# v of pair 0 loaded by units, an earlier first part of W_in, v narrowed on GpSimd, and a last result in three pieces

## The chip, the cores and the metric

The kernel runs on one core of one Trainium2 chip. The core has five engines with instruction streams of their own: TensorE (PE, with its weight loads as PEld), VectorE (DVE), ScalarE (ACT), GpSimd (POOL) and SyncE (SP). SP and POOL issue the DMAs here; 16 DMA engines move the data. The metric is the device time of one execution in microseconds (us). The kernel before takes 178.17 us (median of 4 runs, 178.02 to 178.48).

## The reference

A gated recurrence over 768 steps, for 4 batches and 8 heads of width 48, whose output feeds a two-layer network:

```python
for t in range(S):                                   # B, H, S, D = 4, 8, 768, 48
    state = alpha[:, :, t, :, None] * state + einsum('bhd,bhe->bhde', k[:, :, t], v[:, :, t])
    y[:, :, t] = einsum('bhd,bhde->bhe', q[:, :, t], state)
x = y.transpose(0, 2, 1, 3).reshape(3072, 384)
h = x @ w_in                                         # 384 x 2048
g = 0.5 * h * (1 + tanh(c * (h + 0.044715 * h ** 3)))
out = g @ w_out                                      # 2048 x 384, float32
```

## The kernel before

**Tiling.** The 768 steps are cut into 6 chunks of 128 steps. Two batches of one chunk are a *pair*; there are 12 pairs, numbered 0 to 11 (pairs 0 and 1 are chunk 0, pairs 2 and 3 chunk 1, and so on). One batch of a pair is a *unit*, 0 or 1. For a pair the kernel loads a (alpha), q, k and v, takes the logarithm of a (`ln`), sums it along the steps by a matmul (`cum`), and exponentiates the sums (`b`, `binv`, `bend`). Then q and k are scaled (`qp`, `kp`), turned over on PE (`t`) and copied out of PSUM (`ev`), multiplied (`attn`) and masked (`mask`). `y` is the masked product times v, plus the part that comes from the state; `x` copies it to bf16, `tx` turns it over, `xe` copies that into `xT`. `kv` and `st` carry the state on; from chunk 1 on `st` is two VectorE instructions (L520 adds, L523 multiplies), in chunk 0 it is one. `end` prepares the factor of `st`.

**The two layers.** `l1` (L564) is 6 matmuls of 128x256, 8 such tasks for each pair (`l10.` to `l111.`), and `gelu` (L570) follows on ACT. `l2` (L583) multiplies by W_out, 4 tasks of 4 matmuls of 128x384 for each unit; `ot` (L595) copies the result out of PSUM and `store` (L601) writes it. The tasks `l20.` are the second layer of pairs 0 and 1 together (16 tasks); they begin when all 16 `l1` tasks of these two pairs have been issued. W_in comes in four parts, each read by two `l1` tasks of every pair: part 0 by `l1` 0 and 1, part 1 by 2 and 3, part 2 by 4 and 5, part 3 by 6 and 7. W_out comes in four parts too.

**Packed pairs.** Pairs 0 and 1 are loaded in a layout of their own (q, k and a by unit on SP, L297), so that their `kp` is not in the order that `kv` needs; k is turned back (`t0.4`, `t0.5`, `t1.4`, `t1.5` with their `ev`, L446 and L453). Their v is loaded as float32 (L300) and narrowed to bf16 by `vb` (L381), on ACT or VectorE. Later pairs' v is narrowed by the DMA itself.

**The last unit.** Its second layer is done in two halves of 192 columns, each over all 16 blocks of the inner dimension, in a bank of its own, with its own `ot` and `store` (32 matmuls of 128x192).

**What sets the order.** Everything is a task with dependencies, buffers that it takes, and costs; `Scheduler.order` lays the tasks out on engines, and every engine then runs its own list in order. First it takes the steps of `FIRST`, a list written out by hand (engine:task, `fill.n` being n matmuls on zeros); after that it chooses by due times and by the costs `W`. While it goes through `FIRST` it uses the costs of the table `COST` where that has an entry. `LANDED` holds the due times of the loads, `LOADS` the order in which POOL issues them, and a `gate` is a tiny POOL copy (L306) that holds the POOL queue until a load has landed or a task is done. A POOL load also waits until the eighth load before it on POOL has landed. The PSUM pool `yk` has two buffers, shared by `t`, `kv`, `y` and `tx`; `ff` has four, for `l1`, `l2`, the fills and, in pairs 0 and 1, `cum`.

POOL's order before is: gate on a of pair 0, unit 1; v of pair 0 in one load; gate on `qp` of pair 0, unit 1; W_in part 0; v of pair 1; W_in parts 1, 2, 3; W_out parts 0, 1; then a, q, k, v of the first unit of pair 2; W_out part 2; and so on.

Of the kernel before, what the change touches and what calls it, by code (L numbers as in the profile page):

```python
# [16 lines left out]
    cum=530, cum_packed=1500, t8=450, t4=225, attn=340, kv=170, inter=170, intra=205, tx=168, l1_4=655, l1_2=340, l2=655,  # L17
    qk2=910, qk1=500, ev8=650, ev4=350, mask=640, st=1090, st0=545, end=110, attn2=590, vb=320, vb_act=480, ring=1300, ring_issue=670, out=2050, lead=600, receipt=1400, receipt_hw=1000, xc=520, xe=330, ot=540,
    ev8_act=960, ev4_act=520, xc_act=450, xe_act=450, ot_act=450,
# [5 lines left out]
    ("DVE", "ev"): (605, 115), ("DVE", "kp"): (480, 120), ("DVE", "mask"): (605, 115), ("DVE", "qp"): (480, 120),  # L25
    ("DVE", "st"): (470, 130), ("DVE", "x"): (480, 120), ("DVE", "xe"): (270, 120),
}
LAT = {"SP": 0, "PE": 210, "ACT": 110, "DVE": 90, "POOL": 0}
# [18 lines left out]
class Scheduler:  # L47
# [16 lines left out]
    def order(self):  # L64
        free = {e: 0 for e in LAT}
        taken = {tag: [] for tag in self.bufs}
        table, wire, xbar, head, out = LN_EXP, 0, 0, 0, []
# [26 lines left out]
        def put(t, at, e):  # L94
            nonlocal wire, xbar
            for tag, users in t.takes:
                taken[tag].append(users)
            cost, lat = COST.get((e, t.kind), (t.cost[e], LAT[e])) if fixed else (t.cost[e], LAT[e])
            t.start, t.end, t.engine, t.load = at, at + cost, e, None
            free[e] = t.end  # L100
            t.done = t.end + lat
            if t.name in self.landed:
                t.done = self.landed[t.name]
                if e != "SP":
                    wire = t.done - W["receipt"]
            elif t.land is not None:
                wire = max(wire, t.end + W["lead"]) + t.land
                t.done = wire + W["receipt_hw" if e == "SP" else "receipt"]
            if t.kind in ("turn", "store"):
                xbar = t.done = max(xbar, t.end + W["landed"] - t.xbar) + t.xbar  # L110
                t.done += t.late
            out.append(t)
# [59 lines left out]
class _Kernel:  # L172
# [5 lines left out]
    EARLY = (0, 1)  # L178
    LOADS = ('gatea 0 1', 'v0', 'gateqp 0 1', 'in 0', 'v1', 'in 1', 'in 2', 'in 3', 'out 0', 'out 1', '2a', 'out 2', '2b', 'out 3', '3', '4', '5', '6', '7', '8', '9', '10', '11')

# [3 lines left out]
    FIRST = """  # L184
        A:table.0 S:load.0 S:load.1 S:load.2 S:load.3 S:load.4 A:ln0.0 S:load.5 P:fill.7 P:cum0.0 A:ln0.1 G:gate.0 G:load.12 S:load.6 P:cum0.1 A:b0.0 S:load.7
        A:binv0.0 V:qp0.0 A:bend0.0 A:b0.1 V:kp0.0 S:load.8 P:fill.2 P:t0.0 A:bend0.1 A:binv0.1 V:ev0.0 P:t0.1 S:load.9 A:ev0.1 S:load.10 V:qp0.1 P:fill.3
        P:attn0.0 V:kp0.1 P:t0.2 G:gate.1 S:load.11 G:load.13 V:mask0.1 P:fill.1 P:t0.3 G:load.14 A:ev0.3 V:end0.0 V:ev0.2 A:ln1.0 V:mask0.0 P:fill.4
        P:attn0.1 G:load.15 P:cum1.0 V:mask0.2 A:vb0.0 G:load.16 A:ln1.1 V:vb0.1 P:y0.0 V:mask0.3 A:b1.0 P:cum1.1 G:load.17 A:x0.0 V:qp1.0 A:binv1.0 P:y0.1
        G:load.18 A:b1.1 P:t1.0 V:x0.1 A:bend1.0 G:load.19 A:ev1.0 V:kp1.0 P:fill.2 P:tx0.1 V:xe0.1 A:binv1.1 P:tx0.0 G:load.20 P:t1.1 A:bend1.1 V:xe0.0
        G:load.21 V:qp1.1 P:t0.5 A:ev1.1 V:kp1.1 G:load.22 A:ev0.5 P:fill.1 P:attn1.0 G:load.23 P:t1.3 V:mask1.1 P:t1.2 A:ev1.3 P:l10.0 G:load.24 V:mask1.0  # L190
        A:ev1.2 P:kv0.1 G:load.25 V:end1.0 V:st0.1 P:t0.4 G:load.26 P:attn1.1 A:ev0.4 P:t1.5 G:load.27 A:ev1.5 V:vb1.0 G:load.28 V:mask1.2 P:y1.0 P:l10.1
        G:load.29 A:x1.0 V:mask1.3 A:vb1.1 P:kv0.0 P:tx1.0 G:load.30 V:st0.0 P:l10.3 V:xe1.0 P:y1.1 P:kv1.1 G:load.31 P:l10.2 V:x1.1 A:gelu0.0 V:st1.1 P:tx1.1
        A:gelu0.1 G:load.32 P:l10.4 V:xe1.1 A:gelu0.3 P:l10.5 A:gelu0.2 G:load.33 P:l11.0 A:gelu0.4 A:gelu0.5 P:l11.1 A:gelu1.0 P:l11.2 A:gelu1.1 P:l11.6
        A:gelu1.2 P:l10.6 A:gelu1.6 P:l11.5 A:gelu0.6 P:l11.7 A:gelu1.5 P:l11.4 A:gelu1.7 P:l10.7 A:gelu1.4 P:l11.3 A:gelu0.7 P:t1.4 A:gelu1.3 P:l20.1 V:ev1.4
        P:l20.2 P:kv1.0 P:l20.5
    """.split()
    LANDED = {"load.0": 2800, "load.1": 3400, "load.2": 4400, "load.3": 5100, "load.4": 6750, "load.5": 7300, "load.12": 9850, "load.6": 9000, "load.7":
              10300, "load.8": 10800, "load.9": 11300, "load.10": 11900, "load.11": 12300, "load.13": 14900, "load.14": 17600, "load.15":
              19300, "load.16": 21300, "load.17": 23000, "load.18": 25000, "load.19": 26600, "load.20": 27700, "load.21": 28400, "load.22":
              29000, "load.23": 29400, "load.24": 31300, "load.25": 32100, "load.26": 32700, "load.27": 33300, "load.28": 33800, "load.29":  # L200
              35900, "load.30": 37700, "load.31": 39400, "load.32": 41300, "load.33": 42600}

# [7 lines left out]

    HALVES = ((3, 0), (3, 1), (3, 2), (3, 3), (4, 0))

# [54 lines left out]
    def copy(self, e):  # L267
        return self.nc.scalar.copy if e == "ACT" else self.nc.vector.tensor_copy

# [303 lines left out]
    def layer2(self, f, c, b, part):  # L573
        def emit(e):
            if part == 0:
                f["acc", c, b] = self.tile("ff", [self.C, self.d_model], F32, "acc")
            if part == 2 and (c, b) == (self.NCH - 1, self.B - 1):
                f["acc", c, b] = self.tile("ff", [self.C, self.d_model], F32, "acc")
            last, w = (c, b) == (self.NCH - 1, self.B - 1), self.d_model // 2
            for lo, hi, nts in (((part // 2 * w, part // 2 * w + w, range(part % 2 * 8, part % 2 * 8 + 8)),) if last else  # L580
                                ((0, self.d_model, range(part * 4, part * 4 + 4)),)):
                for nt in nts:
                    self.nc.tensor.matmul(f["acc", c, b][:, lo:hi], self.gT[c % self.NG][:, nt, b * self.C:(b + 1) * self.C],  # L583
                                          self.w_out[:, nt, lo:hi], start=nt == 0, stop=nt == self.NFT - 1,
                                          skip_group_check=last)
            if last:
                f["acc", c, b, part // 2] = f["acc", c, b]
        return emit

    def result(self, f, c, b, half=None):  # L590
        def emit(e):
            if half in (None, 0):
                f["ot", c, b] = self.tile("ot", [self.C, self.d_model], F32)
            sl = slice(0, self.d_model) if half is None else slice(half * self.d_model // 2, (half + 1) * self.d_model // 2)
            self.copy(e)(f["ot", c, b][:, sl], f["acc", c, b] if half is None else f["acc", c, b, half][:, sl])  # L595
        return emit

    def store(self, f, c, b, half=None):
        r = b * self.S + c * self.C
        sl = slice(0, self.d_model) if half is None else slice(half * self.d_model // 2, (half + 1) * self.d_model // 2)  # L600
        return lambda e: self.nc.sync.dma_start(self.out[r:r + self.C, sl], f["ot", c, b][:, sl])  # L601


    def tasks(self):
# [15 lines left out]
        def rows(m, names="aqkv", part="ab"):  # L620
            for lo, hi in ((0, 2),) if m in self.PACKED else self.parts(m):
                if part == "ab"[hi % 2]:
# [33 lines left out]
        for m, (c, i) in enumerate(pairs):  # L656
# [48 lines left out]
            if m in self.NARROW:  # L705
                vin = [s.add("vb", {"DVE": W["vb"], "ACT": W["vb_act"]}, P + 19, self.narrow(u, j, j + 1), vin[j:j + 1]) for j in range(2)]
            if u["sums"]:
# [103 lines left out]
        def layer2(m):  # L811
# [4 lines left out]
            first = {}  # L816
            for u, part in ([(u, part) for part in parts for u in units] if m == 0 else [(u, part) for u in units for part in parts]):
                c, b = u
                t = s.add("l2", {"PE": W["l2"]}, 10000 + n, self.layer2(f, c, b, part),
                          gs[m if m else b // 2][2 * part:2 * part + 2] + [loads["w", "out", part]] + firsts, stream=n - 16)  # L820
                l2s.setdefault(c, []).append(t)
                n += 1
                first.setdefault(u, t)
                if (c, b) == (NCH - 1, B - 1):
# [3 lines left out]
                    if part % 2:  # L828
                        ot = s.add("ot", {"DVE": W["ot"], "ACT": W["ot_act"]}, -1, self.result(f, c, b, part // 2), [t])
                        ots.append((ot, s.add("store", {"SP": W["sp"]}, n, self.store(f, c, b, part // 2), [ot])))  # L830
                        parts_of[part // 2].take("ff", ot)
                        if part == 3:
                            ots[0][0].take("ot", *[x[1] for x in ots])
# [69 lines left out]
```

## Time and profile before

| | |
|---|---|
| median of 4 runs | 178.17 us (178.02 to 178.48) |
| the profiled execution's own time | 178.04 us |
| its span, first to last instruction | 176.3 us |
| granted TensorE clock, mean | 1.000 |
| PE busy | 171.6 us (97%) |
| ACT busy | 131.0 us (74%) |
| DVE busy | 95.0 us (54%) |
| POOL busy | 57.9 us (33%) |

The span is 1.7 us shorter than the execution's own time; this rest lies before the first and after the last instruction. A busy PE is not PE at its peak, because matmuls are pipelined and wait inside their durations; whether it holds the end is read from the chain of waits. All times below are microseconds from the start of the span. A row of the timeline gives the start, the duration, the engine, the line, the operation, the tile written and read, the count of instructions merged, and, in brackets, the idle time before it and what ended it.

### The profile page before, as it was taken

The page shows a single profiled execution, that of the slowest core. Times are in us where ns is not written, and L with a number is a line of the kernel's source. Part 1 is how long each engine was busy: PE and PEld are TensorE (multiplying, and loading weights), DVE is VectorE, ACT ScalarE, POOL GpSimd, SP SyncE. Part 2 cuts the span into 40 slices and gives each one's busy share as a digit, 9 for nine tenths or more (in the row PEclk, how much of TensorE's full clock was granted, in tenths as well). Part 3 has the DMA queues.
Part 4 walks back from the last instruction along what each step waited for, and adds up shares of the span by engine and source line. Part 5 has one row for each costly group of instructions (what it writes and reads, how often), then busy time and mean ns, then how long its engine had stood idle before and what let it go on. Part 6 is the DMA issues. An engine that isn't in the chain of part 4 may idle for free.

```text
span 176.3 us, 4421 instructions
## 1 busy us (share of the span) xinstructions
PE 171.6 (97%) x1833; PEld 135.6 (77%) x1833; DVE 95.0 (54%) x187; ACT 131.0 (74%) x216; POOL 57.9 (33%) x64
## 2 busy tenths in 40 slices
PE   7999999999999999999999999999999999999993
PEld 2666899666986897797698698688697697786972
DVE  6599800354967893696598797495426405000000
ACT  4677899775898668858788967977988984481931
POOL 2397446986746767575720000000000000000000
PEclk9999999999999999999999999999999999999999
DMA  4999999999999999999999992361261360401102
GB/s 119 276 284 203 202 241 233 239 226 203 247 272 199 236 260 214 195 257 201 193 263 228 216 152 73 66 168 48 47 172 42 87 166 4 119 15 48 45 0 89
DMA packets 49620, 28.86 MB, mean 164 GB/s; under 512 B 37568, under 2 KB 46016, under 8 KB 49600
## 3 DMA queue, kind: packets, MB, share of 16 engines
q0 software_dynamic: 26464, 17.70, 60.9%
q1 hardware_dynamic: 23136, 10.88, 25.0%
q8 instruction: 14, 0.23, 0.6%
q14 instruction: 6, 0.05, 0.1%
HBM read 25.17 MB, written 4.72 MB: 170 GB/s over the span
## 4 chain that ended last, share of the span: by engine, by line
PE 88%; ACT 3%; DVE 3%; DMA 2%; SPq 2%; issue 1%; DVEq 0%
PE acc L583 36%; PE hT L564 35%; PE at L481 4%; PE qkT_ps L420 3%; PE yps L538 2%; DMA k<-in_k_dram 2%; PE yps L535 2%; PE cum L370 2%; PE kv L498 2%; SPq L297 2%; DVE atm L488 1%; ACT qkT L438 1%; PE xT_ps L552 1%; ACT L570 1%; PE cum L372 1%
## 5 line engine op out<-in xcount | busy, mean ns | idle before, releaser
L583 PE MATMUL acc<-w_out,gT 128*128 128x384 bf16 (+1 forms) x400 | 69.4, 319 | 0.0
L564 PE MATMUL hT<-xT,w_in 128*128 128x256 bf16 x576 | 68.8, 273 | 0.1
L570 ACT ACTIVATE gT<-hT 128x512 bf16<-128x512 f32 x96 | 56.1, 599 | 15.1 <-PE hT L564 11.6
L564 PEld LDWEIGHTS <-w_in 128*128 128x128 bf16 x576 | 61.2, 113 | 1.5 <-issue 0.2
L583 PEld LDWEIGHTS <-gT 128*128 128x128 bf16 x400 | 36.5, 97 | 18.9
L488 DVE TENSOR_TENSOR atm<-at,ut 128x512 bf16<-128x512 f32 x48 | 30.1, 683 | 13.7 <-PE at L481 13.7
L410 DVE TENSOR_TENSOR qp<-q,b 128x768 bf16<-128x768 f32 (+1 forms) x15 | 11.9, 795 | 17.8 <-ACT b L399 16.2
L595 ACT COPY ot<-acc 128x384 f32<-128x384 f32 (+1 forms) x18 | 8.3, 461 | 13.7 <-PE acc L583 9.4
L300 POOL DMA_DIRECT2D k<-in_k_dram x11 | 12.2, 1107 | 7.6 <-DMA vb<-in_v_dram 2.7
L300 POOL DMA_DIRECT2D q<-in_q_dram x11 | 12.2, 1108 | 6.0 <-DMA k<-in_k_dram 1.4
L300 POOL DMA_DIRECT2D a<-in_alpha_dram x11 | 12.2, 1114 | 5.7 <-DMA w_in<-in_moe_w_in_dram 1.3
L300 POOL DMA_DIRECT2D vb<-in_v_dram x11 | 12.1, 1102 | 5.3 <-DMA a<-in_alpha_dram 2.6
L272 ACT ACT_TABLE_LOAD x9 | 11.5, 1283 | 0.9 <-PEq L887 0.7
L399 ACT ACTIVATE b<-cum 128x768 bf16<-128x768 f32 (+1 forms) x15 | 10.3, 684 | 2.6 <-PE cum L372 1.4
L410 DVE TENSOR_TENSOR kp<-k,binv 128x768 bf16<-128x768 f32 (+1 forms) x15 | 11.9, 791 | 0.0
L570 ACT ACT_TABLE_LOAD x9 | 11.5, 1283 | 0.2
L399 ACT ACTIVATE binv<-cum 128x768 bf16<-128x768 f32 (+1 forms) x15 | 10.2, 680 | 0.0
L520 DVE TENSOR_TENSOR stmp<-kv,st 128x384 f32<-128x384 f32 x16 | 8.8, 553 | 2.0 <-PE kv L498 2.0
L545 DVE CAST x<-yps 128x384 bf16<-128x384 f32 x12 | 6.7, 558 | 5.2 <-PE yps L538 5.2
L353 ACT ACTIVATE la<-a 128x768 f16<-128x768 f32 (+1 forms) x11 | 8.5, 783 | 1.0 <-DMA a<-in_alpha_dram 0.9
L523 DVE TENSOR_TENSOR st<-stmp,ends 128x384 bf16<-128x384 f32 x16 | 8.9, 558 | 0.6
L538 PE MATMUL yps<-vb,atm 128*128 128x48 bf16 x192 | 8.9, 183 | 0.1
(64 smaller groups left out, 155.8 us busy)
## 6 DMA issues: line engine op xcount, KB each, us to landing
a<-in_alpha_dram POOLq DMA_DIRECT2D x9, 384.0 KB, 12.0
q<-in_q_dram POOLq DMA_DIRECT2D x9, 384.0 KB, 11.7
k<-in_k_dram POOLq DMA_DIRECT2D x9, 384.0 KB, 11.7
out_dram<-ot SPq DMA_DIRECT2D x18, 192.0 KB, 6.3
vb<-in_v_dram POOLq DMA_DIRECT2D x9, 192.0 KB, 12.0
w_in<-in_moe_w_in_dram POOLq DMA_DIRECT2D x4, 384.0 KB, 9.1
w_out<-in_moe_w_out_dram POOLq DMA_DIRECT2D x4, 384.0 KB, 11.1
out_dram<-ot SPq DMA_DIRECT2D x12, 96.0 KB, 1.8
```

The costliest lines, as they stand in the source:

```text
L272: nc.scalar.add_instruction(mybir.InstLoadActFuncSet(name=nc.get_next_instruction_name(), act_func_set_id=i, engine=mybir.EngineType.Activ ...
L300: dma(u[t][:, lo:hi].rearrange("t b h d -> t (b h) d"), src.rearrange("b h s d -> s (b h) d")[c * C:(c + 1) * C])
L353: self.nc.scalar.activation(u["la"][:, lo:hi, :, 0:self.D], u["a"][:, lo:hi], AF.Ln)
L399: self.nc.scalar.activation(u[n].rearrange("t i h d -> t i (h d)")[:, lo:hi], cum, AF.Exp, scale=1.0 if n == "b" else -1.0)
L410: self.nc.vector.tensor_tensor(out, rows, b, op=ALU.mult)
L488: self.nc.vector.tensor_tensor(u["atm", i][:, o], u["at", i][o], self.ut[:, None, :].to_broadcast([self.C, self.H // 2, self.C]), op=ALU.mult)
L520: nc.vector.tensor_tensor(s, acc, old, op=ALU.add)
L523: nc.vector.tensor_tensor(new.rearrange("f p (o d) -> f (p o) d", o=2), acc.rearrange("f p (o d) -> f (p o) d", o=2), ends, op=ALU.mult)
L538: nc.tensor.matmul(y[:, h, :], u["atm", i][:, h % 2, h // 2, :], u["vb"][:, i, h, :], start=c == 0, stop=True, skip_group_check=True)
L564: self.nc.tensor.matmul(h[:, s], w_in[:, j, nt % 4 + s], self.xT[c % self.NX][:, j, lo:hi].rearrange("p g t -> p (g t)"), start=j == 0, st ...
L570: return lambda e: self.nc.scalar.activation(self.gT[c % self.NG][:, nt:nt + 2, lo * self.C:hi * self.C], f.pop(("h", c, lo, nt)), AF.Gelu ...
L583: self.nc.tensor.matmul(f["acc", c, b][:, lo:hi], self.gT[c % self.NG][:, nt, b * self.C:(b + 1) * self.C], self.w_out[:, nt, lo:hi], star ...
```

## The change

Five edits, with the order of the work laid out anew:

1. v of pair 0 comes in two loads, one for each unit, and the narrowing of v of pairs 0 and 1 (`vb`, four instructions) is done by POOL alone. All later POOL loads are placed behind these: those from v of pair 1 on behind the two `vb` of pair 0, those from k of pair 2 on behind the two `vb` of pair 1.
2. The second gate waits for the landing of q of pair 0, unit 1, and no more for `qp` of that unit; a third gate, on the landing of a of pair 1, unit 1, stands before v of pair 1. POOL's order becomes: gate; v0 unit 0; v0 unit 1; gate; W_in part 0; `vb0.0`; `vb0.1`; gate; v of pair 1; W_in parts 1, 2, 3; W_out parts 0, 1; a and q of pair 2, first unit; `vb1.0`; `vb1.1`; k and v of that unit; W_out part 2; and so on.
3. `FIRST` is a new list that goes on further, up to `t3.0`, with new due times in `LANDED`; the costs of `COST` no longer apply to tasks of pair 3 and later. Outside `FIRST` the order from about the second layer of pair 3 on is the same on PE as before.
4. The last unit's result is done in pieces of 192, 128 and 64 columns instead of two of 192 (48 matmuls instead of 32, three copies, three stores).
5. The result of chunk 4, batch 0 is stored whole instead of in halves.

In the new order on PE, k of pair 0 is turned back early (`t0.4`, `t0.5` ahead of `y0.0`), the first `l1` stands ahead of `t1.1`, and the second `l1` ahead of `t1.2`. ACT runs the first `gelu` ahead of `x1.0`. On VectorE the stretch around pair 3 is `ot0.3`, `end3.0`, `st2.1`, `qp3.0`, `kp3.0`, `st2.0`, where it was `qp3.0`, `st2.0`, `st2.1`, `kp3.0`, `end3.0`; on PE, four `l1` tasks of pair 2 stand between `kv2` and `t3.0`, where there were six.

```diff
-    LOADS = ('gatea 0 1', 'v0', 'gateqp 0 1', 'in 0', 'v1', 'in 1', 'in 2', 'in 3', 'out 0', 'out 1', '2a', 'out 2', ...
+    LOADS = ('gatea 0 1', 'v0', 'gateq 0 1', 'in 0', 'gatea 1 1', 'v1', 'in 1', 'in 2', 'in 3', 'out 0', 'out 1', '2a', 'out 2', ...
...
-            cost, lat = COST.get((e, t.kind), (t.cost[e], LAT[e])) if fixed else (t.cost[e], LAT[e])
+            cost, lat = COST.get((e, t.kind), (t.cost[e], LAT[e])) if fixed and not 300 <= t.prio < 10000 else (t.cost[e], LAT[e])
...
+        ... A:b1.1 P:fill.1 P:t1.0 G:load.17 P:kv0.0 V:kp1.0 A:ev1.0
+        P:l10.1 G:load.18 V:st0.0 A:binv1.1 P:t1.1 V:end1.0 P:l10.0 V:qp1.1 A:ev1.1 G:load.19 V:kp1.1 P:t1.2 P:attn1.0 G:load.20 A:ev1.2 P:t1.3 V:mask1.0
+        A:ev1.3 P:t1.4 G:load.21 V:mask1.1 G:load.22 P:kv0.1 V:ev1.4 P:attn1.1 G:vb1.0 V:mask1.2 G:vb1.1 P:y1.0 A:gelu0.0 V:st0.1 G:load.23 A:x1.0 P:l10.2
+        V:mask1.3 A:gelu0.1 G:load.24 P:l10.3 G:load.25 P:tx1.0 P:y1.1 V:xe1.0 P:l10.4 G:load.26 A:x1.1 A:gelu0.2 G:load.27 P:t1.5 P:tx1.1 P:l10.5 A:gelu0.3
+        G:load.28 V:xe1.1 V:ev1.5 ... P:l11.0 ... P:l10.7 ... A:gelu1.4 A:gelu1.7 P:kv1.0 P:kv1.1 P:l20.1 ...
+        ... P:l20.15 A:binv3.0 V:xe2.0 P:tx2.1 A:b3.0 P:l20.14 V:xe2.1 P:kv2.1 A:bend3.0 P:kv2.0 A:ot0.2 V:ot0.3 P:l12.0 V:end3.0 V:st2.1 S:store0.2
+        S:store0.3 V:qp3.0 P:l12.1 P:l12.2 V:kp3.0 A:gelu2.0 P:l12.3 A:gelu2.1 V:st2.0 P:t3.0 A:gelu2.2
...
-    HALVES = ((3, 0), (3, 1), (3, 2), (3, 3), (4, 0))
+    HALVES = ((3, 0), (3, 1), (3, 2), (3, 3))
+
+    PIECES = (0, 192, 320, 384)
...
-            if part == 2 and (c, b) == (self.NCH - 1, self.B - 1):
+            last, w = (c, b) == (self.NCH - 1, self.B - 1), self.PIECES
+            if part and part % 2 == 0 and last:
                 f["acc", c, b] = self.tile("ff", [self.C, self.d_model], F32, "acc")
-            for lo, hi, nts in (((part // 2 * w, part // 2 * w + w, range(part % 2 * 8, part % 2 * 8 + 8)),) if last else
+            for lo, hi, nts in (((w[part // 2], w[part // 2 + 1], range(part % 2 * 8, part % 2 * 8 + 8)),) if last else
...
-            for lo, hi in ((0, 2),) if m in self.PACKED else self.parts(m):
+            for lo, hi in ((0, 2),) if m in self.PACKED and names != "v" or m == 1 else self.parts(m):
...
-                vin = [s.add("vb", {"DVE": W["vb"], "ACT": W["vb_act"]}, P + 19, self.narrow(u, j, j + 1), vin[j:j + 1]) for j in range(2)]
+                vin = [s.add("vb", {"POOL": W["vb_pool"]}, P + 19, self.narrow(u, j, j + 1), vin[j:j + 1]) for j in range(2)]
+                for t in loads.values():
+                    if t.prio >= loads[("v", 1, 0) if m == 0 else ("k", 2, 0)].prio and not any(x in t.deps for x in vin):
+                        t.deps += vin
```

## The prediction

> **What bounds the kernel now.** I read the page first (busy shares, slices, the chain that ended last), then the chain in order of time, then the timeline up to 50 us and the tail, then the DMA view of single windows.
>
> ```profile
> PE 171.6 (97%) x1833; PEld 135.6 (77%) x1833; DVE 95.0 (54%) x187; ACT 131.0 (74%) x216; POOL 57.9 (33%) x64
> PEclk9999999999999999999999999999999999999999
> DMA  4999999999999999999999992361261360401102
> PE 88%; ACT 3%; DVE 3%; DMA 2%; SPq 2%; issue 1%; DVEq 0%
> ```
>
> PE carries 88% of the chain at a full clock. The DMA engines are full from the second slice to the 24th. So engine time saved on DVE or ACT is worth nothing by itself; what counts is when PE starts to run without gaps, what work is left then, and gaps behind that.
>
> The chain in order of time (start, length, what):
>
> ```profile
> 20.12 1.28 ACT L570
> ...
> 22.06 8.02 PE hT L564 x72
> 30.08 0.22 PE k_ps L446 x4
> ...
> 44.77 0.22 PE idle L281
> ```
>
> From 22.06 on the chain is PE alone, packed piece to piece up to the last result; one fill (0.22) and the odd tenth are all it loses. Ahead of 22.06 PE waits often. So 22.06, where the first `l1` on W_in part 2 (`l10.4`) starts, is the hinge. Twelve `l1` tasks follow (8.02), then `t1.4` (0.22) and, two `l2` later, `kv1.0` (0.17): the work of pairs 0 and 1 is through at 22.06 + 8.02 + 0.22 + 0.17 = 30.47, the `l2` tasks between left aside.
>
> What holds the hinge: rows of the timeline, then two answers of the DMA view (the issue at 11.95 alone; the window 9 to 11).
>
> ```profile
> 9.28 0.75 POOL L313 DMA_DIRECT2D w_in<-in_moe_w_in_dram  x1
> 10.02 1.18 POOL L300 DMA_DIRECT2D v<-in_v_dram  x1
> 11.20 2.26 POOL L313 DMA_DIRECT2D w_in<-in_moe_w_in_dram  x3
> 21.63 0.33 PE L552 MATMUL xT_ps<-ident,x 128*128 128x128 bf16 x3
> ```
>
> ```profile
> w_in<-in_moe_w_in_dram POOLq DMA_DIRECT2D x1, 384.0 KB, 9.7
> ```
>
> ```profile
> q1 hardware_dynamic: 886, 0.64, 98.7%
> q0 software_dynamic: 24, 0.05, 7.6%
> ```
>
> Part 2 is issued at 11.95 and lands 9.7 later, at 21.6; `tx1.1` (21.63) stands in the PE queue just ahead. Both end together, so neither alone is worth much. Parts 1 and 3, read the same way, land at 19.7 and 23.5: 1.9 apart. Between 9 and 11 POOL's queue q0 moves next to nothing, and the rows that SP issued fill the engines.
>
> **The change part by part.**
>
> *Head, VectorE and ACT.* `ev0.0` and `ev0.2` go from DVE to ACT, the four `vb` (0.51, 0.59, 0.35, 0.53) go to POOL. `y0.0` stood at 11.60 behind `vb0.0`, which ran at 10.77 when all of v0 had landed (4.57 + 6.2). With half of v0 there sooner it waits for `mask0.1` instead, about 10.9. First `l1`: after `xe0.1` and part 0, about 14.5 (was 16.54). All this stands ahead of the hinge, and counts only as far as the hinge moves.
>
> *Loads.* The second gate waits for q of unit 1 (issued 3.50, landed 3.8 later, 7.3) instead of `qp0.1` (8.66), so part 0 is issued at 7.6, not 9.28: 1.7 earlier. SP's queue is not reordered; rows of pair 1 that landed at 11.6, 12.1, 12.7 and 13.2 share the engines with part 0 and come 1 to 2 later, while their `qp` and `kp` now stand at about 13 to 17, so this stays covered (a `qp1.0` 1 later still leaves `l10.1` ahead of the hinge). On POOL, v1 and all behind it wait for `vb0.0`, `vb0.1` and the third gate: v0 unit 1 lands at 10.7 as now, + 0.54 + 0.19 (the gate row) = 11.5, where v1 was issued at 10.02. Behind that wait stand v1, W_in 1 to 3, W_out 0 and 1 and pair 2's rows, all 1.5 later in issue.
>
> When does part 2 land? Bounds: 1.7 earlier (part 0's advance passed on in full) and 1.5 later (the later issue passed on in full). Against the late end: v1 took 7.9 from issue to landing where v0 took 6.2, so the queue, not the issue, was late, and 1.7 of cover is there. Against the early end: the engines are full, and the bytes ahead of part 2 are the same. In between: part 0 now moves in a stretch in which q0 was nearly empty, and parts 1 to 3 have only v1 ahead of them. I take half of the early end, 0.8: landing 20.8, first `l1` on it at 20.95.
>
> The DMA: Bandwidth & Descriptors page of the Trainium skill, section "Issuing engines are not separate DMA queues", says that DMAs from all issuing engines interleave on the same 16 engines, and that issuing elsewhere saves only issue time. The 98.7% above agrees with it. By that rule alone part 2 would land at 21.6 as now, and the sum below would end 0.8 higher.
>
> *GpSimd's narrowing.* The trace has none. From its rows: a one-column copy 0.19, a 128x128 select 0.29, so 0.0008 per column and 0.49 for 384; VectorE's own narrowing took 0.35 and 0.59. I take 0.54; ends 0.35 and 1.2 (twice the slower VectorE row). On the path: v1 issued 11.5 + 1.18 + 2.26 (W_in) + 1.15 (W_out) + 0.93 + 0.90 (a, q of pair 2) = 17.9; v1 landed at 17.9 before; `vb1.0` + 0.54 and 0.15 to PE, 18.6; then `y1.0` 0.20, two `l1` 1.31, `tx1.0` 0.17, `y1.1` 0.20: 20.5. That is the earliest hinge, just below 20.95. Each tenth more for a narrowing moves it by two tenths (`vb0.1` and `vb1.0`).
>
> The GPSIMD Engine Reference of the skill, section "Engine selection", puts elementwise work on VectorE and calls GpSimd about twice as slow for two inputs, one input about as fast. No row here has a narrowing on GpSimd. At twice the mean VectorE row (0.94) the hinge would be at 21.3 and the sum 0.35 higher.
>
> *Work behind the hinge.* Twelve `l1` (8.02), `t1.5` 0.22, `tx1.1` 0.17, `kv1.0` and `kv1.1` 0.34: 8.75, where it was 8.41. The end of pairs 0 and 1: 20.95 + 8.75 = 29.70 against 30.47, **-0.77**.
>
> *Layer 2 of pairs 0 and 1.* The fill at 44.77 is gone: **-0.22**. `cum`, `t`, `attn`, `y` of pair 2 stand elsewhere among the `l2` tasks; each waits for ACT or DVE work that has an `l2` of 0.65 or more in front, so nothing.
>
> *`t3.0`.* VectorE rows of before:
>
> ```profile
> 44.73 0.95 DVE L410 TENSOR_TENSOR qp<-q,b 128x768 bf16<-128x768 f32 x1
> 45.59 0.55 DVE L520 TENSOR_TENSOR stmp<-kv,st 128x384 f32<-128x384 f32 x1
> ...
> 47.72 0.95 DVE L410 TENSOR_TENSOR kp<-k,binv 128x768 bf16<-128x768 f32 x1
> ```
>
> A `st` holds VectorE 1.06 (two of them between 45.59 and 47.72), while the table that laid out the list has 0.47 for it. After: counted from `kv2.1`, VectorE runs `ot0.3` 0.47, `end3.0` 0.12, `st2.1` 1.06, `qp3.0` 0.86, `kp3.0` 0.95, 0.05 to PE: 3.55. PE has two `kv` 0.34 and four `l1` 2.62: 2.96. `t3.0` waits **+0.6**; before, six `l1` covered it to 49.26. Ends: 0 and 1.2 (if `t3.1` also waits for `st2.0` to free its bank). Nothing later can make it up, PE being full.
>
> *Tail.*
>
> ```profile
> 172.12 0.32 ACT L595 COPY ot<-acc 128x192 f32<-128x192 f32 x1 [0.89 <-PE acc L583]
> 173.40 0.32 ACT L595 COPY ot<-acc 128x192 f32<-128x192 f32 x1 [0.96 <-PE acc L583]
> ```
>
> A copy of 384 columns takes 0.48, of 192 0.32, so 64 take 0.21: -0.11. Stores land 1.8 (192 KB) and 1.6 (96 KB) after issue; 32 KB about 1.5: -0.1. The matmuls have 384 columns in total as before; those of 64 take about 0.027 each by the `yps` 128x48 row (8 in 0.20). The second piece's copy and store issue (0.27, 0.33) end as the last copy does. **-0.2**; ends -0.25 and +0.4 (16 short matmuls at the 0.055 of a 128-column one). The whole store of chunk 4 is hidden by 30 us of PE.
>
> **Sum:** -0.77 - 0.22 + 0.6 - 0.2 = **-0.59**. On the profiled execution's 178.04 that is 177.45; this execution is 0.13 below the median 178.17, so the median comes to **177.6**.
>
> **The rivals.**
>
> *Part 2 lands as now.* The full DMA slices speak for it, the empty q0 against. The hinge is 21.75, the end 30.50 (+0.03), the sum +0.2: 178.4.
>
> *Slower: GpSimd holds its own queue.* At 1.5 for a narrowing the hinge is 20.5 + 2 x 0.96 = 22.4, the end 31.15 (+0.68), the sum +0.86: 179.0. It turns the sum above +0.36 from about 1.2 on. For it: POOL is also busy with descriptors, and a one-column cast took 0.36 beside VectorE. Against: the other POOL rows.
>
> *No wait at `t3.0`.* If `kp3.0` is in time the sum is -1.2: 177.0. Against it stands the 1.06.
>
> **How the numbers follow.** A change of 0.2% (0.36 us) is about what can be told here. Forecast 0.50 (its own range 176.9 to 178.0), part 2 unmoved 0.20, slower (GpSimd's queue, and what else delays part 2) 0.25, no wait at `t3.0` 0.05. Faster by over 0.2%: 0.55; within: 0.20; slower: 0.25. The range reaches to 176.8 (earliest hinge, half the wait) and 178.8 (hinge at 22.2).
>
> **What would show it.** First `l1` near 14.5; the first `l1` on part 2 near 21 and no gap of PE after it up to 46; then a PE wait of about 0.6 ended by VectorE's `kp`; a last copy of 0.21. Wrong if part 2 lands after 21.7, if a GpSimd narrowing takes over 1.2, if PE waits in the `l2` tasks, or if the short matmuls pace by weight loads.

## The result and the profile after

The changed kernel takes 178.51 us (median of 53 runs), the kernel before 178.24 us (median of 79 runs beside them). The ratio is 1.0019 with a 95% interval of 1.0009 to 1.0029: slower by 0.2%, where 0.3% faster was forecast. The profiled execution took 178.45 us with a span of 176.6, 0.06 below its median. All ratios leave out executions more than 1.5% above the fastest of the same kernel, among them one of 347.8 us in the run early below.

The page of the changed kernel, the lines that answer to those shown of before (busy time, granted clock, DMA share by slice, the chain by engine):

```profile
PE 170.4 (96%) x1843; PEld 135.0 (76%) x1843; DVE 94.0 (53%) x185; ACT 129.9 (74%) x215; POOL 60.7 (34%) x70
PEclk9999999999999999999999999999999999999999
DMA  4999999999999999999999993262261360301102
PE 80%; DMA 12%; DVE 2%; POOL 2%; issue 1%; ACT 1%; SPq 0%; ACTq 0%; POOLq 0%
```

The DMA part of the chain was 2%, and it is now 12%. PE has less work and a longer span. Two pieces of that chain carry it. The first is the head, in order of time (start, length, what):

```profile
13.26 8.36 DMA w_in<-in_moe_w_in_dram
21.61 0.05 issue
21.66 0.85 PE hT L570 x6
...
22.90 7.20 PE hT L570 x66
30.10 0.34 PE kv L504 x8
30.44 2.60 PE acc L589 x16
```

W_in part 2 is issued at 13.26 (11.93 before) and lands at 21.62, where it landed at 21.64 before. The hinge is at 21.66, 0.40 earlier than 22.06, but `t1.5` (0.22) and `tx1.1` (0.17) now stand behind it, so the last `l1` of pairs 0 and 1 ends at 30.10, as before (30.08). The second piece has no counterpart in the chain of before, which is PE alone there:

```profile
96.40 0.97 ACT L278
97.37 4.69 DMA xT<-x
102.06 0.04 issue
102.10 0.81 PE hT L570 x6
```

The second transposed x of pair 6 lands at 102.06. Before, it landed at 100.95, and PE came to it at 101.55, 0.60 later. PE's rows of the timeline, before and then after:

```profile
98.95 2.76 PE L583 MATMUL acc<-w_out,gT 128*128 128x384 bf16 x16
101.55 0.82 PE L564 MATMUL hT<-xT,w_in 128*128 128x256 bf16 x6
```

```profile
99.11 2.76 PE L589 MATMUL acc<-w_out,gT 128*128 128x384 bf16 x16
102.10 0.81 PE L570 MATMUL hT<-xT,w_in 128*128 128x256 bf16 x6 [0.23 <-DMA xT<-x]
```

From the start of the `acc` to the `l1` it is 2.60 before and 2.99 after. (The bracket counts from the modelled end of the `acc`, which the next matmul overlaps when it does not wait.)

To see where the 0.38 us come from (176.26 to 176.64, unrounded), I follow the same work in both traces:

| what ends or starts | before | after | difference | gained or lost since the row above |
|---|---|---|---|---|
| last `l1` of pairs 0 and 1 ends | 30.08 | 30.10 | +0.02 | |
| first `kv` of pair 2 starts, fill gone | 44.83 | 44.58 | -0.25 | -0.27 |
| `acc` x16 ahead of pair 6 starts | 98.95 | 99.11 | +0.16 | +0.41, `t3.0` and `t3.1` |
| next `acc` starts, behind the `l1` of pair 6 | 109.23 | 109.78 | +0.55 | +0.39, transposed x |
| last store lands | 175.35 | 175.74 | +0.39 | -0.16, tail |

GpSimd's narrowings and the issues behind them, POOL's rows of after:

```profile
6.95 0.75 POOL L319 DMA_DIRECT2D w_in<-in_moe_w_in_dram  x1
9.09 0.51 POOL L387 CAST vb<-v 128x384 bf16<-128x384 f32 x1 [1.39 <-DMA v<-in_v_dram]
10.75 0.51 POOL L387 CAST vb<-v 128x384 bf16<-128x384 f32 x1 [1.16 <-DMA v<-in_v_dram]
11.21 0.19 POOL L312 COPY gate<-a 128x1 f32<-128x1 f32 x1
11.33 1.19 POOL L306 DMA_DIRECT2D v<-in_v_dram  x1
12.52 2.26 POOL L319 DMA_DIRECT2D w_in<-in_moe_w_in_dram  x3
```

Part 0 is issued 2.33 earlier than before (9.28); all behind it is issued 1.31 later. What that does to PE shows in a table by stage. Its columns are busy time and count of PE, PEld, DVE, ACT and POOL, granted clock, DMA share and GB/s. (The share adds up the packets' times, which overlap, so it can pass 1.) First before, then after:

```profile
12.00:14.00 2.00, 1.84 (x27) 1.34 (x26) 2.00 (x5) 1.80 (x6) 2.00 (x3) 1.00 1.21 195
18.00:22.00 4.00, 3.95 (x61) 3.48 (x61) 3.53 (x9) 3.84 (x7) 1.84 (x3) 1.00 1.23 203
```

```profile
12.00:14.00 2.00, 1.97 (x32) 1.50 (x29) 1.68 (x4) 2.00 (x8) 2.00 (x3) 1.00 1.16 264
18.00:22.00 4.00, 2.87 (x42) 2.53 (x42) 2.31 (x5) 3.02 (x6) 2.50 (x5) 1.00 1.17 178
```

PE does work earlier (the first `l1` starts at 14.26, 16.54 before) and then idles 1.13 of the four microseconds from 18 to 22, where it had idled 0.05. The DMA engines move more than before at 12 to 14 and less at 18 to 22, with about the same high busy share. The landings show where the advance goes: v of pair 1 lands at 17.47 (17.94 before) and part 1 at 19.23 (19.73), about 0.5 earlier, but part 2 comes 2.38 behind part 1 where it came 1.91 behind, and part 3 lands at 23.95 (23.55).

Around `t3.0`, PE and then DVE in the timeline of after:

```profile
47.54 0.39 PE L426 MATMUL qkT_ps<-ident,qp 128*128 128x128 bf16 x4
47.89 0.40 PE L426 MATMUL qkT_ps<-ident,kp 128*128 128x128 bf16 x4
48.36 0.38 PE L426 MATMUL qkT_ps<-ident,qp 128*128 128x128 bf16 x4
48.58 0.39 PE L426 MATMUL qkT_ps<-ident,kp 128*128 128x128 bf16 x4
48.80 1.47 PE L570 MATMUL hT<-xT,w_in 128*128 128x256 bf16 x12
```

```profile
46.88 0.95 DVE L416 TENSOR_TENSOR kp<-k,binv 128x768 bf16<-128x768 f32 x1
47.75 0.55 DVE L526 TENSOR_TENSOR stmp<-kv,st 128x384 f32<-128x384 f32 x1
```

`t3.0` waits for `kp3.0` (0.13) and `t3.1` for the bank that `st2.0` reads (0.24): 1.26 from `t3.0` to the next `l1`, 0.89 before (49.10 to 49.99). The tail, ACT's rows:

```profile
172.67 0.32 ACT L601 COPY ot<-acc 128x192 f32<-128x192 f32 x1 [0.89 <-PE acc L589]
173.52 0.27 ACT L601 COPY ot<-acc 128x128 f32<-128x128 f32 x1 [0.53 <-PE acc L589]
173.99 0.21 ACT L601 COPY ot<-acc 128x64 f32<-128x64 f32 x1 [0.20 <-PE acc L589]
```

### The profile page after: what moved, and what is told of

It reads as the page before. It is cut to its first block, busy times and chain, and to the rows that moved or that the text cites. A ratio compares the mean times of both kernels' runs of the same rounds, so it can differ in the third digit from the quotient of the medians.

```text
span 176.6 us, 4439 instructions
## 1 busy us (share of the span) xinstructions
PE 170.4 (96%) x1843; PEld 135.0 (76%) x1843; DVE 94.0 (53%) x185; ACT 129.9 (74%) x215; POOL 60.7 (34%) x70
## 4 chain that ended last, share of the span: by engine, by line
PE 80%; DMA 12%; DVE 2%; POOL 2%; issue 1%; ACT 1%; SPq 0%; ACTq 0%; POOLq 0%
PE hT L570 33%; PE acc L589 32%; DMA w_in<-in_moe_w_in_dram 5%; PE at L487 3%; DMA xT<-x 3%; DMA v<-in_v_dram 3%; PE qkT_ps L426 2%; PE yps L544 2%; PE yps L541 2%; PE cum L376 2%; PE kv L504 2%; DMA a<-in_alpha_dram 2%; PE xT_ps L558 1%; POOL v L306 1%; PE cum L378 1%
## 5 line engine op out<-in xcount | busy, mean ns | idle before, releaser
L589 PE MATMUL acc<-w_out,gT 128*128 128x384 bf16 (+3 forms) x416 | 69.0, 313 | 0.0
L589 PEld LDWEIGHTS <-gT 128*128 128x128 bf16 x416 | 37.0, 97 | 19.2
L601 ACT COPY ot<-acc 128x384 f32<-128x384 f32 (+3 forms) x17 | 7.5, 440 | 11.4 <-PE acc L589 11.2
L278 ACT ACT_TABLE_LOAD x9 | 11.5, 1283 | 0.9 <-PEq L904 0.7
L576 ACT ACT_TABLE_LOAD x9 | 11.5, 1283 | 0.2
L551 ACT CAST x<-yps 128x384 bf16<-128x384 f32 x14 | 6.7, 478 | 4.3 <-PE yps L544 4.3
L444 ACT COPY qkT<-qkT_ps 128x512 bf16<-128x512 bf16 (+1 forms) x11 | 7.7, 708 | 2.8 <-PE qkT_ps L426 2.7
```

What stands on the lines that cost most here:

```text
L278: nc.scalar.add_instruction(mybir.InstLoadActFuncSet(name=nc.get_next_instruction_name(), act_func_set_id=i, engine=mybir.EngineType.Activ ...
L444: self.copy(e)(t, ps)
L576: return lambda e: self.nc.scalar.activation(self.gT[c % self.NG][:, nt:nt + 2, lo * self.C:hi * self.C], f.pop(("h", c, lo, nt)), AF.Gelu ...
```

## The experiments

All are timed against the kernel before on the same chip, and the ratio is to that. One kernel's runs spread over about 1.5 us, so a median of 12 runs is good to about 0.25%. A profile is one of those runs, and mechanisms are read from it; where its own time is far from the median, I say so. A difference to the changed kernel is the difference of the two ratios to the kernel before, 1.0019 being the changed kernel's.

A single landing varies from execution to execution. The head of the changed kernel stands unaltered in order_l1, hold and hold2 as well, and in these four profiles part 2 lands at 21.62, 21.93, 22.86 and 21.60. With the head of gate_a0, which all3 and best share, it lands at 20.98, 21.00 and 21.52; with the head of before, which extra and pieces share, at 21.64, 22.25 and 21.39. So a few tenths between two profiles show little by themselves.

### Does W_in part 2 depend on when the loads are issued?

**gate_qp**: the second gate as before.

```diff
-    LOADS = ('gatea 0 1', 'v0', 'gateq 0 1', 'in 0', ...
+    LOADS = ('gatea 0 1', 'v0', 'gateqp 0 1', 'in 0', ...
```

> The changed kernel, with the second gate on qp0.1 as in the kernel before, so that W_in's first part is issued at about 9.3 us instead of 6.95 and nothing else is changed. Theory (the DMA engines are full, the bytes ahead of W_in part 2 are the same, so its landing does not depend on when part 0 is issued): part 0 lands 1 to 1.5 later, rows of pair 1 earlier, part 2 still within 0.3 of 21.6 and the first layer-1 task on it within 0.3 of 21.66; time within 0.3 of the changed kernel, 178.3 to 178.8. Rival (the step of the prediction: half or all of the advance of part 0 is passed on to part 2): part 2 lands 0.8 to 2.3 later, time 179.2 or more.

Measured: ratio 1.0036 (1.0011 to 1.0062), median 178.89. In the profile part 0 is issued at 9.34 and lands at 16.20, part 2 lands at 23.40, 1.8 later than in the changed kernel, and the first `l1` on it starts at 23.45. That is what the rival expected of the profile. But this execution took 179.86, the slowest of its 12, hold's profile has part 2 at 22.86 with the changed kernel's head, and the times (1.0036 and 1.0019, medians 0.4 apart) are not told apart. So this run alone leaves open what the earlier issue of part 0 is worth.

**gate_a0**: the other half. Nothing behind part 0 waits for v of pair 0, and the third gate opens earlier.

```diff
-    LOADS = (..., 'gateq 0 1', 'in 0', 'gatea 1 1', 'v1', ...
+    LOADS = (..., 'gateq 0 1', 'in 0', 'gatea 1 0', 'v1', ...
-        ... G:vb0.0 ... G:vb0.1 ...
+        ... A:vb0.0 ... V:vb0.1 ...
-    vin = [s.add("vb", {"POOL": W["vb_pool"]}, P + 19, ...
+    vin = [s.add("vb", {"POOL": W["vb_pool"], **({} if m else {"DVE": 320, "ACT": 480})}, P + 19, ...
```

> The changed kernel, with the third gate on the first half of alpha of pair 1 (landed 9.5 us) instead of the second (10.7), and v of pair 0 narrowed by ScalarE and VectorE as in the kernel before, so that no load on GpSimd's queue waits for v of pair 0. v1 and W_in parts 1 to 3 are then issued 1.4 us earlier, at about 9.9 to 11.8, behind a part 0 that is still issued at 7. Theory (both shifts of issue are passed on almost in full, part 0's advance as gain and the later issue behind it as loss, and they cancelled): W_in part 2 lands at 19.9 to 20.6 instead of 21.6, the first layer-1 task on it starts at 20.5 to 21, time 0.6 to 1.0 below the changed kernel, 177.7. Rival (the engines are full and only the bytes ahead of part 2 count): part 2 still lands within 0.3 of 21.6, time within 0.2 of the changed kernel, 178.5; or, with rows of pair 1 landing later still, slower.

Measured: ratio 0.9967 (0.9936 to 0.9997), median 177.88, so 0.5% below the changed kernel. POOL's rows:

```profile
8.02 0.75 POOL L319 DMA_DIRECT2D w_in<-in_moe_w_in_dram  x1 [0.28 <-issue]
9.67 1.18 POOL L306 DMA_DIRECT2D v<-in_v_dram  x1 [0.29 <-issue]
10.85 2.28 POOL L319 DMA_DIRECT2D w_in<-in_moe_w_in_dram  x3
```

Its stages 18 to 22:

```profile
18.00:22.00 4.00, 3.67 (x54) 3.12 (x52) 3.21 (x7) 3.63 (x7) 2.65 (x4) 1.00 1.21 210
```

Part 2, issued at 11.58, lands at 20.98, and the first `l1` on it starts at 21.25 behind other PE work, not behind the load. The landing lies between the two expectations (19.9 to 20.6; 21.3 to 21.9); the time is the theory's. PE is busy 3.67 of the four microseconds instead of 2.87, and the DMA engines move 210 GB/s instead of 178. The issue of v1 hangs on the landing of the first half of a of pair 1, which varies: in the three profiles with this head v1 is issued at 9.67, 10.92 (all3) and 11.28 (best).

**narrow_old**: of the two waits in front of v1, the narrowing alone is taken away. As gate_a0, but with the gate left:

```diff
-    LOADS = (..., 'gatea 1 0', 'v1', ...
+    LOADS = (..., 'gatea 1 1', 'v1', ...
```

> The changed kernel with v of pair 0 narrowed by ScalarE and VectorE, and the third gate left on the second half of alpha of pair 1. Of the two waits ahead of v1 this takes away the narrowing alone. Theory (alpha's second half lands within 0.3 of v's, so either wait holds v1): v1 is issued at 11.0 to 11.3 instead of 11.33, W_in part 2 lands at 21.3 to 21.9, time within 0.25 of the changed kernel, 178.3 to 178.7. Rival (GpSimd's narrowing by itself was the loss): time as with the earlier gate, 177.9.

Measured: ratio 1.0014 (0.9991 to 1.0038), median 178.65: as the changed kernel. v1 is issued at 11.20 (a of pair 1, unit 1, landed at 10.61). GpSimd's narrowing was not the loss by itself; it stood beside a gate that opens at the same time. The profile is of an execution 2 us above its median, with part 2 at 22.86, so its landing does not test the 21.3 to 21.9; it comes back in the last section.

**early**: both edits of gate_a0, the one of order_l1 below, and a third gate that opens earlier still.

```diff
-    LOADS = (..., 'gatea 1 0', 'v1', ...
+    LOADS = (..., 'gatek 0 1', 'v1', ...
```

> The run that joins both edits (v of pair 0 narrowed by ScalarE and VectorE, two more layer-1 tasks ahead of t3.0), with the third gate on k of unit 1 of pair 0 (landed 7.7 to 8.5 us) instead of alpha of pair 1 (9.1 to 10.7), so that v1 is issued at about 8.6 and W_in part 2 at about 10.5. Theory (whatever holds GpSimd's loads in the first 12 us comes back at W_in part 2 and again at the end of the stream): part 2 lands at 20.3 to 21, the last load lands by 99.3, TensorE waits no more than 0.1 for x of pair 6 at 101, time 177.3 or less. Rival (rows of pair 1 then share the engines for longer, q and k of its unit 1 land after 15.5 instead of 15, and the y of pair 1 holds TensorE in place of part 2): TensorE's first layer-1 task on part 2 no earlier than 21.5, time 177.7 or more.

Measured: median 177.73, ratio 0.9996 (0.9967 to 1.0025; two executions over 179 hold it up). The profiled execution (177.36) issues v1 at 8.82 and part 2 at 10.73; part 2 lands at 21.03, the last load at 98.53, the second x of pair 6 at 100.16, and PE starts on it at 101.04 without a wait. Rows of pair 1 land up to 16.00 and hold up nothing on PE. So against gate_a0's profile 0.85 of further advance in issue brought no earlier landing of part 2, and all3's profile has it at 21.00 with an issue at 12.83: the engines behind the rows of pairs 0 and 1 seem to allow about 21.0, and the issue of part 2 alone does not set its landing. By its time it is not told apart from the kernel before.

### The wait at t3.0

**order_l1**: two more `l1` ahead of it.

```diff
-    ... P:l12.3 A:gelu2.1 V:st2.0 P:t3.0 A:gelu2.2
+    ... P:l12.3 A:gelu2.1 P:l12.4 V:st2.0 A:gelu2.2 P:l12.5 P:t3.0
```

> The changed kernel, with two more layer-1 tasks of pair 2 (l12.4, l12.5) ahead of t3.0 on TensorE. Theory: the two t tasks of pair 3 take 0.89 from first to next instruction as in the kernel before, instead of 1.26, and all behind comes 0.37 earlier, so the span is 0.3 to 0.4 shorter: 178.15. Rival (the wait is VectorE's work and only moves: TensorE then waits for ev3, mask3 or a bank behind it): less than 0.1 gained, 178.45.

Measured: ratio 1.0003 (0.9981 to 1.0026), median 178.39. PE's rows:

```profile
45.23 4.09 PE L570 MATMUL hT<-xT,w_in 128*128 128x256 bf16 x36
49.16 0.39 PE L426 MATMUL qkT_ps<-ident,qp 128*128 128x128 bf16 x4
...
50.05 0.71 PE L570 MATMUL hT<-xT,w_in 128*128 128x256 bf16 x5
```

0.89 from `t3.0` to the next `l1`, as before. Between the first `kv` of pair 2 and the `acc` ahead of pair 6 this run is 0.4 shorter than the changed kernel: the mechanism as expected. In the time no more than 0.16% shows, which the interval can't tell from the expected 0.2% or from nothing.

### The wait for x of pair 6

**hold**: the last three loads are kept back.

```diff
+    HELD = (6, 1)
...
+    def wait_x(self, c, b):
+        return lambda e: self.nc.gpsimd.tensor_copy(self.gate[:, 0:1], self.xT[c % self.NX][:, 0, b, 0:1])
...
+                if (m, j) == self.HELD:
+                    g = s.add("gate", {"POOL": 150}, loads["v", 11, 0].prio - 1, self.wait_x(c, b), [xe])
+                    for r in "vqk":
+                        loads[r, 11, 0].deps.append(g)
```

> The changed kernel, with the last three loads on GpSimd's queue (q, k and v of pair 11, 0.96 MB of reads) held until the second transposed x of pair 6 has landed; before, they were issued at 86 to 90 us. Theory (the loss of 0.39 at 102 us is the two transposes of x sharing the DMA engines with loads that land up to 100.5): the second xT lands by 100.5 instead of 102.06, TensorE does not wait ahead of the first layer-1 task of pair 6, and the time is 0.3 to 0.4 below the changed kernel: 178.15. Rival 1 (the transposes are late for their own sake, by their issue on SP or their source): xT still lands near 102, time as the changed kernel, 178.5. Rival 2 (the held loads then fall on the transposes of pair 7, which land after 112): the wait comes back there, 178.5 or more.

Measured: ratio 1.036 (1.032 to 1.040), median 185.08. The second x of pair 6 lands 2.3 after its issue (99.90 to 102.21) instead of 4.7, and PE does not wait for it. But the three loads, issued from 102.88 on, fall on x of pair 7 (issued at 110.44, landed at 116.89), as the second rival had it, and on q and k of pair 8, which had not been thought of. (The profiled execution is 2.3 above the median; its head is late and its clock low there, so only the transposes are read from it.) From the DMA view at 105, and PE's waits behind 90 us:

```profile
vb<-in_v_dram POOLq DMA_DIRECT2D x1, 192.0 KB, 11.6
qkT<-qp SPq DMA_TRANSPOSE x1, 6.0
qkT<-kp SPq DMA_TRANSPOSE x1, 9.9
```

```profile
PE at L492 <- DMA qkT<-kp: 4.3, 1, 4.3
```

Both halves say the same: with the engines free a transposition of x takes 2.3 and one of q or k 2.7; beside these loads x took 6.4 and k 9.9. The waits are not the whole cost: behind them the granted clock is 0.50 from 116 to 120, where it is 1.00 in the changed kernel.

**hold2**: kept back until x of pair 7 has landed.

```diff
-    HELD = (6, 1)
+    HELD = (7, 1)
```

> The changed kernel, with the last three loads of GpSimd's queue held until the second transposed x of pair 7 has landed (about 112 us), so that they fall between the transposes of pair 8 and those of pair 9, not on any. Theory (the loss of 0.39 at 102 us is transposes sharing the DMA engines with loads still under way, and the 9.95 us of one transpose in the run held until pair 6 was the held loads falling on it): no TensorE wait at 102 and none behind it, time 0.3 to 0.45 below the changed kernel, 178.1. Rival (something else holds the transposes, or TensorE finds another wait there): 178.5.

Measured: ratio 1.0271 (1.0217 to 1.0326), median 183.22. No wait at 102 again (x issued 97.36, landed 99.68). The loads, released at 112, fall on x and on q and k behind it: x of pair 8, issued at 111.91 and 113.37, takes 4.6 and 5.8, q and k of pair 9, issued at 115.78 and 117.34, take 7.3 and 6.5, and PE waits 2.8 for the last. Behind that wait the granted clock is 0.50 from 124 to 126, which adds to the cost. I had taken the gap ahead of the next transposes to be free, and it was not.

**extra**: the kernel before with one more load, to bring about the wait on purpose.

```diff
+        self.spare = const.tile([C, H, D], F32, name="spare")
...
+                    if (r, m) == ("v", 6):
+                        s.add("more", {"POOL": 550}, n, self.more, [loads[r, m, lo]])
...
+    def more(self, e):
+        self.nc.gpsimd.dma_start(self.spare.rearrange("t h d -> t h d"), self.src["q"][0].rearrange("h s d -> s h d")[:self.C])
```

> The kernel before, with one more load of 192 KB on GpSimd's queue behind v of pair 6, into a tile that nobody reads. Theory (GpSimd's loads are one full stream up to 100 us, and transposes of x behind its end are late when it is): every later load lands 0.9 later, the last at about 100.2 instead of 99.33, the second x of pair 6 at about 101.8 instead of 100.95, and TensorE waits 0.1 to 0.3 for it at 101.7, where the kernel before has no wait. Rival (there is slack in the stream, or the transposes don't depend on it): the second x still lands within 0.2 of 100.95, no wait.

Measured: one run of 178.45. The last load lands at 100.27 (expected 100.2) and the second x of pair 6 at 101.88 (101.8). PE itself is 0.27 late in this execution from the head on, and still loses 0.11 to the kernel before between 101 and 109; had it come at 101.55, as in the kernel before, it would have been 0.33 ahead of the landing. The loss is the small end of what was expected, by that accident.

Put together with the other runs: in ten of the eleven kernels with nothing held, the second x of pair 6 lands 1.5 to 1.6 after GpSimd's last load, whatever its issue (93.4 to 95.8 for the first of the two). In the eleventh, narrow_old, PE was 2.8 late in the profile, the first x was issued at 96.66, behind most of the loads, and the second took 2.3.

| kernel | last load lands | second x lands | PE lost between 101 and 109 |
|---|---|---|---|
| before | 99.33 | 100.95 | - |
| extra | 100.27 | 101.88 | 0.11 |
| changed | 100.48 | 102.06 | 0.39 |
| order_l1 | 100.54 | 102.01 | 0.43 |
| gate_a0 | 98.93 | 100.57 | 0 |
| early | 98.53 | 100.16 | 0 |

### The last result in pieces

**pieces**: the kernel before with that part alone (`PIECES` in the change's diff, and what uses it).

```diff
+    PIECES = (0, 192, 320, 384)
```

> The kernel before, with the last result in three pieces (192, 128, 64 columns) and nothing else changed. Theory (the tail term of the prediction was right): the last copy takes 0.21 us instead of 0.32, the last store lands about 0.1 sooner, the matmuls of the last unit take no more than 0.05 longer in total; time 0.2 below the kernel before, 178.0. Rival (32 short matmuls more cost TensorE as much as the pieces save): the last copy starts 0.2 later, time within 0.1 of the kernel before, 178.2.

Measured: ratio 1.0009 (0.9988 to 1.0029), median 178.52, not told apart from no change. In the profile the copies take 0.32, 0.27 and 0.21 and the last store lands 0.16 sooner counted from the last whole copy (4.43 behind its start against 4.59), as in the changed kernel. In this one profile the end of the span lies 1.34 behind that landing instead of 0.91; in the changed kernel and the ten others with pieces it lies 0.90 to 0.93 behind.

### Together

**all3**: gate_a0, order_l1 and hold2 in one.

> The changed kernel with three edits together: v of pair 0 narrowed by ScalarE and VectorE with the third gate on the first half of alpha, two more layer-1 tasks ahead of t3.0, the last three loads held until x of pair 7 has landed. If the gains are separate they add up: 0.4 (t3.0) + 0.4 (transposes) + 0 to 0.8 (head) below the changed kernel, 176.9 to 177.7, and below the kernel before. Rival (a gain ahead of 100 us is given back there, because the loads on GpSimd's queue don't end earlier when TensorE does): no more than 0.4 in all, 178.1.

Measured: ratio 1.025 (1.0213 to 1.0286), median 183.30. Up to 101 us the gains do add up (0.86 ahead of the kernel before), then the held loads cost what they cost in hold2, a wait of PE and a granted clock of 0.50 from 124 to 126 behind it.

**best**: gate_a0 and order_l1 in one, nothing held.

> The changed kernel with two of the edits: v of pair 0 narrowed by ScalarE and VectorE with the third gate on the first half of alpha, and two more layer-1 tasks ahead of t3.0; nothing held. Theory (the head's gain of the run with that gate alone, a landmark 0.27 ahead of the kernel before at 101 us, and the 0.4 of t3.0 add up, and the loads end early enough for the transposes of x): landmarks 0.65 ahead of the kernel before from 67 us on, no TensorE wait of over 0.2 at 101, time 0.3 to 0.4 below that run, 177.5. Rival (TensorE 0.4 earlier at 101 meets the transposes, which come no earlier): 0.2 to 0.4 is lost there, 177.85.

Measured: ratio 0.9961 (0.9937 to 0.9986), median 177.68. In the profile v1 is issued only at 11.28 (a of pair 1 landed at 10.69 here), the last load lands at 99.94, PE is 0.35 ahead at 101 and loses 0.37 there: the rival, in this execution. It is 0.06% below gate_a0, which is nothing that can be told.

**best_k**: the same with the second gate on k of unit 0.

```diff
-    LOADS = ('gatea 0 1', 'v0', 'gateq 0 1', 'in 0', ...
+    LOADS = ('gatea 0 1', 'v0', 'gatek 0 0', 'in 0', ...
```

> As the run that joins both edits, with the second gate (W_in's first part) on k of unit 0 of pair 0 (landed 5.9 us) instead of q of unit 1 (6.4 to 7.4), so that part 0 is issued at about 6.4 instead of 7 to 8. Theory (the issue of part 0 is passed on almost in full): part 2 lands 0.5 to 1 earlier, at about 20.3, time 0.2 to 0.5 lower, 177.2. Rival (q and k of unit 1 of pair 0 then land later and hold the first attention, or the y of pair 1 holds TensorE instead of part 2): the same or slower, 177.5 to 178.

Measured: ratio 0.9950 (0.9932 to 0.9968), median 177.66: below both kernels, by 0.5% and 0.7%. Part 0 is issued at 6.93, not 6.4, and part 2 lands at 21.39, not 20.3; the chain has the same piece again:

```profile
95.76 0.94 ACT L278
96.70 4.72 DMA xT<-x
101.42 0.04 issue
```

PE, 0.48 ahead at 101, loses 0.40 of it there.

## Why the prediction was wrong

**The step that failed** is the landing of part 2: "I take half of the early end, 0.8: landing 20.8". It landed at 21.62, and the hinge came at 21.66 instead of 20.95. The rows ahead of it were right: part 0 issued at 6.95 (7.6), v of pair 0, unit 1 at 10.70 (10.7), a narrowing 0.51 (0.54), v1 issued at 11.33 (11.5), first `l1` at 14.26 (14.5). What was wrong is the argument against the late end, that the later issue had "1.7 of cover". The cover held for v1 and for part 1, which landed 0.5 earlier than before; it did not hold for part 2, which came 2.38 behind part 1, where the prediction had read the parts as 1.9 apart. gate_a0 takes the later issue away: part 2 comes 1.89 behind part 1, at 20.98, and the time goes down by 0.5%; narrow_old, which differs by the gate alone, loses that again. That the earlier part 0 is a gain is read from gate_a0 against the kernel before: part 0 is issued 1.26 earlier there, v1 0.35, part 2 lands 0.66 earlier, and the time is 0.3% lower, while the change's other terms nearly cancel (-0.27 + 0.41 - 0.16); gate_qp's time could not tell. So both shifts count, with opposite signs, the later issue by the times of three kernels and the earlier part 0 by this one comparison; halving the one and dropping the other was no estimate. Why the parts come further apart when they are issued later stays open. The term of -0.77 became -0.03 in the prediction's own count (30.10 + 0.34 against 30.47), and +0.02 at the last `l1`: 0.74 of the 0.97 by which the sum missed.

**The rival "part 2 lands as now"** gave +0.2 and 178.4, with the hinge at 21.75; measured +0.38 in the span, 178.51 and 21.66. It had the right outcome, though its reason (full engines) is half of it: narrow_old and gate_a0 differ by one gate, and by 0.5% in time. The skill's rule that was weighed there, that DMAs from all engines share the same 16 engines and issuing elsewhere saves only issue time (DMA: Bandwidth & Descriptors, "Issuing engines are not separate DMA queues"), gave the right number for this change; gate_a0, where the same queue was issued earlier by 1.7 and gained, shows that the moment of issue on one queue did count here.

**What the prediction did not see** is +0.39 at 102 us, a term that it put at nothing. It read from the chain that PE is alone behind 22.06, and so took all that is off the chain there to be covered. The cover was 0.60 (x of pair 6 landed at 100.95, PE came at 101.55), and it depends on when GpSimd's last load lands, 100.48 instead of 99.33, of which 0.40 was there when W_in part 3 landed (23.95 against 23.55). `extra` shows the dependence in the kernel before, hold and hold2 from the other side. The same page of the skill (DMA: Bandwidth & Descriptors, "Queues, rings and completion order") says that an engine goes round the queues that have work, one whole packet at a time; that fits transposes that come late while loads are under way, but no run here varied the packets.

**`t3.0`**: +0.6 forecast, 0.37 measured (0.13 for `kp3.0`, 0.24 for the bank), between the ends 0 and 1.2. VectorE had begun `ot0.3` 0.18 ahead of `kv2.1`, not behind it, and the first half of `t3.0`, on `qp3.0`, ran during the wait that the sum gave to all of it. (VectorE's terms there add up to 3.51, not 3.55, which changes little.)

**The fill** (-0.22): -0.27 for the stretch, right; the other 0.05 is `t1.4` and `kv1.1`, which the prediction counted in the head. **The tail** (-0.2): -0.16, right; by itself it is below what the times can tell. **GpSimd**: the one-input rate was right, and its rival (1.5 for a narrowing) is out. That agrees with the skill's rule for one input (GPSIMD Engine Reference, "Engine selection").

**The sum** of what was measured: +0.02 - 0.27 + 0.41 + 0.39 - 0.16 = +0.39, where -0.59 was forecast. The time lies in the range given, 176.8 to 178.8, but that is partly luck: its upper end was there for a late hinge, and the wait at 102 us had no place in it.

## What to carry to other kernels

In a stretch where the DMA engines are full, an earlier issue of one load can be bought with a later issue of others: add up both over the queue, and do not offset the one by a cover that was not measured. Where small transfers follow a long stream of loads, look up how much later they may land before the busiest engine waits, since that margin is nowhere in the chain of waits; here it was 0.60 us in 176. A load that is put off comes down somewhere else: both places tried here cost more than ten times what the wait had (4.7 and 6.6 against 0.39), part of it by the clock behind the new waits.

## What the runs showed of the hardware that was not expected

- A DMA transpose of x took 2.3 us from issue to landing with the engines free. Beside the end of the loads of GpSimd's queue the second x of pair 6 took 3.5 to 4.7 in ten kernels, and it landed 1.5 to 1.6 after the last load rather than a fixed time after its own issue; beside held loads transposes took 4.6 to 9.9.
- How early the loads behind part 0 are issued went with the rate of the engines later: at 18 to 22 us they moved 203 GB/s (before), 210 (gate_a0) and 211 (early) with v1 issued at 10.02 or sooner, and 178 with v1 issued at 11.33, at a busy share of 1.17 to 1.23 in all four. The other ten profiles fit: 205 and 208 with v1 issued at 10.01 and 9.63 (extra, pieces), 175 to 192 with v1 issued at 10.76 or later (eight profiles). The runs don't show why.
- In narrow_old's profile PE waited 1.13 us for W_in part 1, and then the same 12 matmuls that take 1.50 in the changed kernel took 2.62:

```profile
20.99 2.62 PE L570 MATMUL hT<-xT,w_in 128*128 128x256 bf16 x12 [1.13 <-DMA w_in<-in_moe_w_in_dram]
```

```profile
20.00:25.00 5.00, 4.01 (x30) 3.20 (x31) 1.18 (x3) 1.64 (x5) 2.18 (x3) 0.66 1.14 200
```

The granted clock was 0.66 from 20 to 25 us, and 0.50 from 22 to 24; hold's profile shows the same two figures there, and hold, hold2 and all3 show 0.50 again behind their long waits for q and k. The skill says that a clock gate lets through half of TensorE's clock pulses or all of them, by how busy TensorE has been of late (TensorE: Matmul & The Clock Gate, "What's actually happening"); the 0.50 behind idle stretches agrees. gate_qp, which waited 0.96 for the same part, kept a clock of 1.00, so one such wait does not decide it. That the idle time which the change added ahead of the hinge makes such a drop more likely is argued, not shown.
